# Attention times v in plain float32 on two column halves of the array, in a fused attention and MoE kernel

## The chip, the cores and the metric

The kernel runs on one core of a Trainium2 chip. The metric is device time in microseconds (us), from the start of the program to its end, taken over several runs and given as a median. A profile of one execution goes with it; its times are read from the hardware profiler's trace.

## The reference

Three layers follow each other. The change is in the first, in the last line of the first function.

```python
def _attn_ref(q, k, v):                       # (4, 12, 448, 64) each
    scores = scale * np.matmul(q, k.transpose(0, 1, 3, 2)) - np.log(S)
    attn = 1.0 / (1.0 + np.exp(-scores))      # a sigmoid, no row sum
    return np.matmul(attn, v).astype(np.float32)

def _moe_ref(x, w1, w2, w3, w_out):           # x: 1792 x 768
    h = np.maximum(np.maximum(x @ w1, x @ w2), x @ w3)
    return (h @ w_out).astype(np.float32)

def _moe2_ref(x, w_in, w_out, g_ln):          # x @ w_in: 1792 x 1024
    ...                                       # h * softmax(h), layer norm, @ w_out
```

All inputs are float32 (the weights arrive as 64-bit floats and are turned into float32 on the chip).

## The kernel before

**Precision.** TensorE multiplies here in float32r, a form of float32 with a short mantissa. To keep float32 accuracy the kernel splits an operand into a rounded part (`copy`, L50/L52) and what is left (`rest`, L55), and adds the products of the parts in PSUM.

**Attention.** There are 24 pairs of heads (`pr`), 6 for each of 4 batches. The 448 keys of a pair are cut into four chunks `c` of 128 rows; the last chunk has 64 new keys and 64 that repeat. `prep_qk` and `prep_v` split k, q and v. `scores` (L350) makes the scores of one chunk for both heads: three products (hi·hi, hi·lo, lo·hi) per head, each head on one 64-row half of the array, 6 matmuls of 448 columns. `sig` (L366) takes the sigmoid on ScalarE and writes the weights `sf`. `attn_split` (L371) splits them into `ah` and `al`; for chunk 3 the rest is written into the upper half of `ah` itself, over the repeated keys. `attend` (L384) multiplies with v: the stationary operand `vt` holds v's rounded part in 64 columns and its rest in the other 64, so that one matmul makes two products, and `ah` and `al` are streamed through it one after the other. That is 4 matmuls of 448 columns for chunks 0 to 2 (two heads, two parts) and 2 for chunk 3, 14 in all for a pair, into one PSUM tile per head. After chunk 3 the two column halves of each tile are added (`sbt` on ScalarE, L406, then `xs` on VectorE, L407), and the sum is split again into `xh` and `xl` (L411, L412) for the next layer.

**Order of the work.** TensorE's order is written out by hand in the loop at L438 over 49 half-steps `hs`: scores of two chunks, a piece of other matmuls (`fill`), `attend` of two chunks of the half-step before, another piece of fill. So there are 48 groups of `attend`, by turns 8 and 6 matmuls, each between pieces of fill. The fill is `gen_w` first (L265, tiles `pw`: the product of two weight matrices, 216 matmuls of 512 columns), and then `gen_g1` (L300, tiles `pg`: x times w1, w2, w3, 324 matmuls of 448 columns for a batch). The order on ScalarE, VectorE and the DMA queue of SyncE is made by a scheduler from the dependences. Weights are loaded as raw 64-bit data (`raw`, three buffers), turned into float32 (`to_f32`: `y`) and split (`wih`/`wil`, `r_wo`, `r_w`). After the attention come the second layer's product (`h`, L539), the norm, transposes of its result (`pt`, L572, the one plain float32 operation on TensorE) and the output product (`po`, L588).

Of the kernel before, what the change touches and what calls it, by code (L numbers as in the profile page):

```python
# [7 lines left out]
F32 = mybir.dt.float32  # L8
F32R = mybir.dt.float32r
I32 = mybir.dt.int32  # L10
AF = mybir.ActivationFunctionType
ALU = mybir.AluOpType
# [4 lines left out]
P = 128  # L17
B, H, S, D = 4, 12, 448, 64
SX = S + D
NPAIR = H // 2  # L20
# [13 lines left out]
def sigmoid_attention_max_moe_solu_ln(tc, q, k, v, w123, wo, wi, w2, g, out):  # L34
# [11 lines left out]
    pe, act, dve, pool, sp = nc.tensor, nc.scalar, nc.vector, nc.gpsimd, nc.sync  # L46

    def copy(eng, dst, src):
        if eng is act:
            act.copy(dst, src)  # L50
        else:
            eng.tensor_copy(dst, src)  # L52

    def rest(eng, dst, src, hi):
        eng.tensor_tensor(out=dst, in0=src, in1=hi.bitcast(F32), op=ALU.subtract)  # L55

    def open_pool(name, bufs, side="left", space=None):
        kw = dict(name=name, bufs=bufs, side=side)
        if space is not None:
            kw["space"] = space  # L60
        cm = tc.tile_pool(**kw)
        return cm, cm.__enter__()
# [13 lines left out]
    a_cm, apool = open_pool("apool", 2)  # L76
    ps1 = [open_pool("ps_sc", 2, space=PSUM), open_pool("ps_av", 2, space=PSUM), open_pool("ps_f", 2, space=PSUM)]
    ps_sc, ps_av, ps_f = (p for _, p in ps1)
# [13 lines left out]
    def run_bg(n=1):  # L92
        while n > 0 and bg:
            if next(bg[0], "end") == "end":
                bg.popleft()
            else:
                n -= 1
# [106 lines left out]


    NP = NPAIR * B
    qk_raw, v_raw, qk_ops, v_ops = {}, {}, {}, {}
    pq = deque()

    def run_pq(n=1):  # L210
# [13 lines left out]
    def load_v(pr):  # L224
        if pr >= NP:
            return
        vr = apool.tile([P, 2, 4, D], F32, tag="vr", name=f"vr{pr}", bufs=1)
        sp.dma_start(out=vr, in_=v[pr])
        v_raw[pr] = vr

    def prep_qk(pr):
        if pr >= NP:
            return []
        qr, kr = qk_raw.pop(pr)
        kt = apool.tile([P, 2, SX], F32R, tag="kt", name=f"kt{pr}")
        qt = apool.tile([P, 2, S], F32R, tag="qt", name=f"qt{pr}")
        qk_ops[pr] = (qt, kt)
        return [
            lambda: copy(dve, kt[:, 0], kr),
            lambda: copy(act, qt[:, 0], qr),  # L240
            lambda: rest(dve, kt[:, 1], kr, kt[:, 0]),
            lambda: rest(dve, qt[:, 1], qr, qt[:, 0]),
            lambda: load_qk(pr + 1),
        ]

    def prep_v(pr):
        if pr >= NP:
            return []
        vr = v_raw.pop(pr)
        vt = apool.tile([P, 2, 4, 2, D], F32R, tag="vt", name=f"vt{pr}")  # L250
        v_ops[pr] = vt
        return [
            lambda: copy(act, vt[:, :, :, 0], vr),
            lambda: rest(dve, vt[:, :, :, 1], vr, vt[:, :, :, 0]),
            lambda: load_v(pr + 1),
        ]


    def group(ps, terms):
# [37 lines left out]
    xs_hi, xs_lo, hts = {}, {}, {}  # L297
# [47 lines left out]
                run_bg()  # L345


    aw = {}

    def scores(pr, c):  # L350
        qt, kt = qk_ops[pr]
        sc = ps_sc.tile([P, 2, 512], F32, tag="sc", name=f"sc{pr}_{c}")
        terms = ((0, 0), (0, 1), (1, 0))
        for t, (x, y) in enumerate(terms):
            for j in range(2):
                rows = slice(j * D, (j + 1) * D)
                pe.matmul(  # L357
                    sc[:, j, :S],
                    lhsT=kt[rows, x, c * P : (c + 1) * P],
                    rhs=qt[rows, y],  # L360
                    start=(t == 0),
                    stop=(t == len(terms) - 1),
                )
        return sc

    def sig(pr, c, sc):  # L366
        sf = apool.tile([P, 2, S], F32, tag="sf", name=f"sf{pr}_{c}", bufs=2)
        act.activation(sf, sc[:, :, :S], AF.Sigmoid, bias=bias_s, scale=1.0 / math.sqrt(D))  # L368
        return sf

    def attn_split(pr, c, sf):  # L371
        ah = apool.tile([P, 2, S], F32R, tag="ah", name=f"ah{pr}_{c}", bufs=4)
        copy(dve if c == 3 and pr >= 2 * NPAIR else act, ah, sf)
        if c < 3:
            al = apool.tile([P, 2, S], F32R, tag="al", name=f"al{pr}_{c}", bufs=3)
            rest(dve, al, sf, ah)
            aw[(pr, c)] = (ah, al)
        else:
            rest(dve, ah[D:], sf[D:], ah[D:])
            aw[(pr, c)] = (ah,)  # L380

    pas = {}

    def attend(pr, c):  # L384

        b, hp = divmod(pr, NPAIR)
        vt = v_ops[pr]
        if c == 0:
            pas[pr] = [ps_av.tile([P, 512], F32, tag="av", name=f"av{pr}_{j}") for j in range(2)]
        parts = aw.pop((pr, c))  # L390
        for j in range(2):
            for i, t in enumerate(parts):
                pe.matmul(  # L393
                    pas[pr][j][:, :S],
                    lhsT=vt[:, j, c].rearrange("p a d -> p (a d)"),
                    rhs=t[:, j],
                    start=(c == 0 and i == 0),
                    stop=(c == 3),
                )
        if c < 3:  # L400
            return
        sbt = apool.tile([P, S], F32, tag="sbt", name=f"sbt{pr}", bufs=1)
        xs = apool.tile([P, S], F32, tag="xs", name=f"xs{pr}", bufs=1)
        for j, pa in enumerate(pas.pop(pr)):
            mine, other = slice(j * D, (j + 1) * D), slice((1 - j) * D, (2 - j) * D)
            act.copy(sbt[mine], pa[other, :S])  # L406
            dve.tensor_tensor(out=xs[mine], in0=pa[mine, :S], in1=sbt[mine], op=ALU.add)  # L407
        if hp == 0:
            xs_hi[b] = (xp0, xp1)[b % 2].tile([P, KC, S], F32R, tag="xh", name=f"xh{b}")
            xs_lo[b] = (xp0, xp1)[b % 2].tile([P, KC, S], F32R, tag="xl", name=f"xl{b}")  # L410
        copy(act if b < 2 else dve, xs_hi[b][:, hp], xs)  # L411
        rest(dve, xs_lo[b][:, hp], xs, xs_hi[b][:, hp])  # L412
        qk_ops.pop(pr)
        v_ops.pop(pr)
        if hp == NPAIR - 1:
            x_done.add(b)
# [8 lines left out]
    for op in prep_qk(0) + prep_v(0):  # L425
        op()
# [11 lines left out]
    for hs in range(HS + 1):  # L438
        pr, h = divmod(hs, 2)
        if hs <= 2 * NPAIR:  # L440
            total = W_MM * max(0, hs - 1) // (2 * NPAIR - 1)
        else:
            total = W_MM + RATE * (hs - 2 * NPAIR)
        todo = total - done
        done = total
        cuts = [todo * i // 4 for i in range(5)]
        parts = [cuts[i + 1] - cuts[i] for i in range(4)]
        mine = [(pr, c) for c in (2 * h, 2 * h + 1)] if hs < HS else []
        scs = [scores(*x) for x in mine]
        sfs = [sig(*x, sc) for x, sc in zip(mine, scs)]  # L450
        if hs < HS:
            pq.extend(prep_v(pr + 1) if h else prep_qk(pr + 1))
        for x, sf, n in zip(mine, sfs, parts):
            attn_split(*x, sf)
            if hs < 2:
                run_bg(9)
            run_pq(2)
            fill(n)
        if hs == HS:
            fill(sum(parts))  # L460
        if hs > 0:
            for c in (2, 3) if h == 0 else (0, 1):
                attend(pr - (h == 0), c)
        fill(parts[2])
        run_pq(len(pq))
        if hs < HS:
            fill(parts[3])
# [32 lines left out]
    n = 0  # L500
# [119 lines left out]
def _layout(i):  # L620
    import numpy as np

    def bits(a):
        return np.ascontiguousarray(a).view(np.int64)

    def pairs(a):

        return a.reshape(B * NPAIR, 2, S, D).transpose(0, 1, 3, 2).reshape(B * NPAIR, P, S)

    f = np.ascontiguousarray  # L630
    k = pairs(i["k"])
    v = i["v"].reshape(B * NPAIR, 2, S, D)
    v = np.concatenate([v, v[:, :, S - D :]], axis=2).reshape(B * NPAIR, 2, 4, P, D).transpose(0, 3, 1, 2, 4)
    w = np.stack([i["moe_w1"], i["moe_w2"], i["moe_w3"]]).reshape(3, KC, P, FC, P)
    return {
        "q": f(pairs(i["q"])),
        "k": f(np.concatenate([k, k[..., S - D :]], axis=2)),
        "v": f(v),
        "w123": bits(w.transpose(3, 0, 2, 1, 4).reshape(NG, P, U)),
        "wo": bits(i["moe_w_out"].reshape(FC, P, KC, P).transpose(0, 3, 2, 1).reshape(FC, P, U)),  # L640
        "wi": bits(
            i["moe2_w_in"].reshape(KC, P, 2, 512).transpose(2, 1, 0, 3).reshape(2, P, 4, U).transpose(0, 2, 1, 3)
        ),
        "w2": bits(i["moe2_w_out"].reshape(K2, P, DM)),
        "g": f(i["moe2_g_ln"].reshape(K2, P).T),
    }
# [19 lines left out]
```

## Time and profile before

| | |
|---|---|
| median of 3 runs | 741.26 us (740.29 to 741.61) |
| profiled execution, its span (no other time of it is recorded) | 740.2 us |
| TensorE matmuls busy | 715.0 us, 97% of the span, 3712 instructions |
| TensorE weight loads busy | 619.9 us |
| VectorE busy | 448.3 us, 734 instructions |
| ScalarE busy | 380.5 us, 596 instructions |

The profile gives, for one execution, the busy time of each engine, groups of like instructions, what each engine waited for, and the instructions in order of time. PE is TensorE, PEld its weight loads, ACT ScalarE, DVE VectorE, SPq the DMA queue of SyncE. A matmul's duration in a row contains its way through the array; how often one can follow another is read from the starts.

### The profile page before, as it was taken

What the parts mean: (1) busy time and instruction counts of PE and PEld (TensorE: products, weight loads), DVE (VectorE), ACT (ScalarE), POOL (GpSimd) and SP (SyncE); (2) the same over time, 40 slices, a digit from 0 to 9 for tenths busy, and PEclk for the clock granted to TensorE, in tenths of its full rate; (3) what the DMA queues carried; (4) which work ended last, traced back from release to release, by engine and by line L of the source; (5) the groups of instructions that cost most, each with busy time, mean ns of one, the idle gap of its engine ahead of it and who ended that gap; (6) DMA issues with size and microseconds to landing.
All of it is one profiled execution on the core that took longest, in us unless ns stands there. A gap on an engine that the chain in (4) does not pass through costs nothing.

```text
span 740.2 us, 9584 instructions
## 1 busy us (share of the span) xinstructions
PE 715.0 (97%) x3712; PEld 619.9 (84%) x3712; DVE 448.3 (61%) x734; ACT 380.5 (51%) x596; POOL 19.6 (3%) x37
## 2 busy tenths in 40 slices
PE   5699989999999999999999999999999999999998
PEld 3478767878888888888888899988999999999997
DVE  5999989999866666665555451269444444444330
ACT  6889989888865555555555250164333222222121
POOL 0010112000000000000000000000000000000000
PEclk9699999999999999999999999999999999999999
DMA  8787899888855566555543589820000000000011
GB/s 285 235 275 231 267 357 324 310 299 307 316 191 185 170 195 200 183 174 181 186 165 128 162 291 420 319 85 1 23 22 21 22 22 22 22 22 22 25 40 44
DMA packets 31438, 124.89 MB, mean 169 GB/s; under 512 B 3616, under 2 KB 6944, under 8 KB 30624
## 3 DMA queue, kind: packets, MB, share of 16 engines
q1 hardware_dynamic: 27072, 103.83, 40.8%
q0 software_dynamic: 4320, 20.45, 7.6%
q8 instruction: 29, 0.48, 0.3%
q14 instruction: 17, 0.14, 0.0%
HBM read 98.31 MB, written 25.95 MB: 168 GB/s over the span
## 4 chain that ended last, share of the span: by engine, by line
PE 78%; ACT 7%; DVE 7%; DMA 4%; issue 4%; SPq 0%; POOL 0%; DVEq 0%; ACTq 0%; POOLq 0%
PE pg L262 32%; PE po L588 16%; PE h L539 16%; PE av L393 6%; PE sc L357 6%; DMA raw<-in_wi 2%; ACT sf L368 2%; PE pt L572 2%; ACT ah L50 1%; DVE r_w L55 1%; PE pw L262 1%; DVE al L55 1%; DMA qr<-in_q 1%; DMA w_d<-ws 1%; ACT y_w L141 1%
## 5 line engine op out<-in xcount | busy, mean ns | idle before, releaser
L262 PE MATMUL pg<-xh,r 128*128 128x448 f32 x648 | 190.5, 369 | 0.0
L262 PEld LDWEIGHTS pg<-xh,r 128*128 128x128 f32 x648 | 121.7, 188 | 16.3 <-issue 4.0
L55 DVE TENSOR_TENSOR al<-sf,ah 128x896 fp32r<-128x896 f32 x72 | 78.3, 1090 | 82.3 <-ACT ah L50 82.0
L368 ACT ACTIVATE sf<-sc,bias_s 128x896 f32<-128x896 f32 x96 | 95.8, 1004 | 54.0 <-PE sc L357 54.0
L262 PE MATMUL pg<-xl,r 128*128 128x448 f32 x324 | 118.3, 365 | 0.0
L539 PE MATMUL h<-wf,hh 128*128 128x512 f32 x336 | 103.9, 390 | 0.0
L357 PE MATMUL sc<-qt,kt 64*128 64x448 f32 x576 | 76.3, 396 | 10.4 <-DVE kt L55 4.7
L50 ACT CAST ah<-sf 128x896 fp32r<-128x896 f32 x84 | 78.2, 943 | 1.7
L357 PEld LDWEIGHTS sc<-qt,kt 64*128 64x128 f32 x576 | 52.2, 192 | 30.7 <-issue 10.8
L588 PE MATMUL po<-w2h,lh 128*128 128x384 f32 x224 | 76.2, 340 | 0.0
L551 DVE TENSOR_REDUCE st<-h 128x1 f32<-128x1024 f32 x14 | 17.1, 1224 | 96.7 <-PE h L539 96.7
L588 PE MATMUL po<-w2h,ll 128*128 128x384 f32 x224 | 75.2, 336 | 0.0
L588 PE MATMUL po<-w2l,lh 128*128 128x384 f32 x224 | 75.2, 336 | 0.0
L539 PEld LDWEIGHTS h<-wf,hh 128*128 128x128 f32 x336 | 62.8, 188 | 12.5
L393 PE MATMUL av<-ah,vt 128*128 128x448 f32 x192 | 68.5, 377 | 0.4 <-DVE xs L407 0.4
L262 PE MATMUL pg<-xh,r_w 128*128 128x448 f32 x216 | 65.2, 373 | 0.5 <-DVE ws L55 0.5
L539 PE MATMUL h<-wf,hl 128*128 128x512 f32 x168 | 65.6, 391 | 0.0
L262 PEld LDWEIGHTS pg<-xl,r 128*128 128x128 f32 x324 | 60.9, 188 | 4.5
L262 PE MATMUL pw<-wih,r_wo 128*128 128x512 f32 x144 | 48.2, 411 | 8.0 <-ACT r_wo L50 5.8
L50 ACT CAST hh<-h 128x128 fp32r<-128x128 f32 x84 | 18.3, 296 | 72.4 <-PE h L539 70.5
L393 PE MATMUL av<-al,vt 128*128 128x448 f32 x144 | 53.6, 372 | 0.9 <-DVE al L55 0.9
L325 ACT COPY s<-pg 128x448 f32<-128x448 f32 x24 | 12.8, 534 | 71.8 <-PE pg L262 71.8
(81 smaller groups left out, 1013.4 us busy)
## 6 DMA issues: line engine op xcount, KB each, us to landing
r<-w_d SPq DMA_DIRECT2D x54, 768.0 KB, 4.4
raw<-in_w SPq DMA_DIRECT2D x26, 768.0 KB, 6.3
w_d<-r_w POOLq DMA_DIRECT2D x18, 768.0 KB, 4.7
kr<-in_k SPq DMA_DIRECT2D x24, 256.0 KB, 2.8
raw<-in_wi SPq DMA_DIRECT2D x8, 768.0 KB, 6.5
vr<-in_v SPq DMA_DIRECT2D x24, 256.0 KB, 3.0
w_d<-ws POOLq DMA_DIRECT2D x12, 512.0 KB, 4.6
wf<-w_d SPq DMA_DIRECT2D x6, 1024.0 KB, 9.8
```

What stands on the lines that cost most here:

```text
L50: act.copy(dst, src)
L55: eng.tensor_tensor(out=dst, in0=src, in1=hi.bitcast(F32), op=ALU.subtract)
L141: act.activation(y, raw.bitcast(F32)[:, :, 1], AF.Prelu, scale=2.0**-112, alpha=2.0**32)
L262: pe.matmul(ps, lhsT=l, rhs=r, start=(i == 0), stop=(i == n - 1))
L325: act.copy(s[:, :S], ps[:, :S])
L357: pe.matmul(sc[:, j, :S], lhsT=kt[rows, x, c * P : (c + 1) * P], rhs=qt[rows, y], start=(t == 0), stop=(t == len(terms) - 1),)
L368: act.activation(sf, sc[:, :, :S], AF.Sigmoid, bias=bias_s, scale=1.0 / math.sqrt(D))
L393: pe.matmul(pas[pr][j][:, :S], lhsT=vt[:, j, c].rearrange("p a d -> p (a d)"), rhs=t[:, j], start=(c == 0 and i == 0), stop=(c == 3),)
L539: pe.matmul(ps[:, n], lhsT=l, rhs=r, start=(f == 0 and i == 0), stop=(f == FC - 1 and i == 2))
L551: dve.tensor_reduce(out=nmax, in_=ps, axis=AX.XY, op=ALU.max, negate=True)
L572: pe.transpose(ps[:, kc], u[:, kc * P : (kc + 1) * P], ident)
L588: pe.matmul(ps[:, :hw], lhsT=l, rhs=r, start=(kc == 0 and i == 0), stop=(kc == K2 - 1 and i == 2))
```

## The change

`attend` takes v as it was loaded (`vr`) and the sigmoid's output `sf` as it was written, both plain float32. Each head's matmul has 64 stationary columns and writes one half (64 partitions) of a single PSUM tile, so both heads of the pair share a tile and each has one column half of the array. There are 2 matmuls for each chunk, 8 for a pair. The splits of v and of the weights, and the sum of the two column halves, are gone; `xh` and `xl` are made from PSUM, `xh` always on ScalarE. `vr` has three buffers in place of one, `sf` five in place of two. The repeated rows of v are zeros now.

```diff
     def load_v(pr):
...
-        vr = apool.tile([P, 2, 4, D], F32, tag="vr", name=f"vr{pr}", bufs=1)
+        vr = apool.tile([P, 2, 4, D], F32, tag="vr", name=f"vr{pr}", bufs=3)
...
     def prep_v(pr):
-        vt = apool.tile([P, 2, 4, 2, D], F32R, tag="vt", name=f"vt{pr}")
-        return [
-            lambda: copy(act, vt[:, :, :, 0], vr),
-            lambda: rest(dve, vt[:, :, :, 1], vr, vt[:, :, :, 0]),
-            lambda: load_v(pr + 1),
-        ]
+        return [lambda: load_v(pr + 1)]
...
-        sf = apool.tile([P, 2, S], F32, tag="sf", name=f"sf{pr}_{c}", bufs=2)
+        sf = apool.tile([P, 2, S], F32, tag="sf", name=f"sf{pr}_{c}", bufs=5)
...
-    def attn_split(pr, c, sf):
-        ah = apool.tile([P, 2, S], F32R, tag="ah", name=f"ah{pr}_{c}", bufs=4)
-        copy(dve if c == 3 and pr >= 2 * NPAIR else act, ah, sf)
-        if c < 3:
-            al = apool.tile([P, 2, S], F32R, tag="al", name=f"al{pr}_{c}", bufs=3)
-            rest(dve, al, sf, ah)
-            aw[(pr, c)] = (ah, al)
-        else:
-            rest(dve, ah[D:], sf[D:], ah[D:])
-            aw[(pr, c)] = (ah,)
...
     def attend(pr, c):
...
-            pas[pr] = [ps_av.tile([P, 512], F32, tag="av", name=f"av{pr}_{j}") for j in range(2)]
+            pas[pr] = ps_av.tile([P, 512], F32, tag="av", name=f"av{pr}")
+        pa = pas[pr]
+        sf = weights.pop((pr, c))
         for j in range(2):
-            for i, t in enumerate(parts):
-                pe.matmul(
-                    pas[pr][j][:, :S],
-                    lhsT=vt[:, j, c].rearrange("p a d -> p (a d)"),
-                    rhs=t[:, j],
-                    start=(c == 0 and i == 0),
-                    stop=(c == 3),
-                )
+            pe.matmul(pa[j * D : (j + 1) * D, :S], lhsT=vr[:, j, c], rhs=sf[:, j], start=(c == 0), stop=(c == 3))
...
-        for j, pa in enumerate(pas.pop(pr)):
-            mine, other = slice(j * D, (j + 1) * D), slice((1 - j) * D, (2 - j) * D)
-            act.copy(sbt[mine], pa[other, :S])
-            dve.tensor_tensor(out=xs[mine], in0=pa[mine, :S], in1=sbt[mine], op=ALU.add)
...
-        copy(act if b < 2 else dve, xs_hi[b][:, hp], xs)
-        rest(dve, xs_lo[b][:, hp], xs, xs_hi[b][:, hp])
+        pas.pop(pr)
+        copy(act, xs_hi[b][:, hp], pa[:, :S])
+        rest(dve, xs_lo[b][:, hp], pa[:, :S], xs_hi[b][:, hp])
```

On TensorE, a group of `attend` with chunks 2 and 3 of a pair, in the middle of the attention. Before (number behind a name: the buffer; `pg` is fill, `x2` two matmuls of the same tiles):

```order
L262 MATMUL pg_5_2485<-xh_1309,r_5_2270 128x448 x2
L393 MATMUL av_0_2412<-ah_2_2384,vt_2224 128x448
L393 MATMUL av_0_2412<-al_2_2386,vt_2224 128x448
L393 MATMUL av_1_2413<-ah_2_2384,vt_2224 128x448
L393 MATMUL av_1_2413<-al_2_2386,vt_2224 128x448
L393 MATMUL av_0_2412<-ah_3_2400,vt_2224 128x448
L393 MATMUL av_1_2413<-ah_3_2400,vt_2224 128x448
L262 MATMUL pg_5_2485<-xl_1310,r_5_2270 128x448
```

The same place now (`64x448` is the output, 64 partitions of one tile for each head):

```order
L253 MATMUL pg_5_2048<-xl_1082,r_5_1872 128x448
L253 MATMUL pg_5_2048<-xh_1081,r_5_1872 128x448 x2
L371 MATMUL av_1988<-sf_2_1965,vr_1714 64x448 x2
L371 MATMUL av_1988<-sf_3_1967,vr_1714 64x448 x2
L253 MATMUL pg_5_2048<-xl_1082,r_5_1872 128x448
```

Six or eight matmuls have become four, head 0 then head 1 of each chunk, at the same place among the fill.

On ScalarE near the start, where the first piece `r_wo` of the weights for the fill is made (`qt` is the copy of the q of the pair after next, which needs its load). Before:

```order
L141 ACTIVATE y_wo_220<-raw_163 128x768
L368 ACTIVATE sf_0_260<-sc_0_246,bias_s 128x896
L50 CAST wih_2_179<-y_wi_3_183 128x768
L50 CAST ah_0_266<-sf_0_260 128x896
L50 CAST qt_265<-qr_190 128x448
L50 CAST r_wo_226<-y_wo_220 128x768
```

And now:

```order
L359 ACTIVATE sf_0_234<-sc_0_220,bias_s 128x896
L359 ACTIVATE sf_1_236<-sc_1_227,bias_s 128x896
L50 CAST wih_2_168<-y_wi_3_172 128x768
L141 ACTIVATE y_wo_204<-raw_156 128x768
L141 ACTIVATE y_wo_245<-raw_166 128x768
L50 CAST r_wo_210<-y_wo_204 128x768
L50 CAST qt_239<-qr_179 128x448
```

`r_wo` stood behind that `qt` and stands ahead of it now; the copies `ah` between them are gone.

## Rows read from the trace of the kernel before

**Rows 1.** The page: busy time and share of each engine; TensorE's granted clock by slices.

```profile
PE 715.0 (97%) x3712; PEld 619.9 (84%) x3712; DVE 448.3 (61%) x734; ACT 380.5 (51%) x596; POOL 19.6 (3%) x37
PEclk9699999999999999999999999999999999999999
```

**Rows 2.** Busy time by stretch: us; PE, PEld, DVE, ACT, POOL; PE clock, DMA share, GB/s.

```profile
0.00:40.00 40.00, 23.63 (x90) 16.47 (x91) 30.18 (x43) 30.62 (x40) 1.59 (x8) 0.83 0.73 251
40.00:108.00 68.00, 63.97 (x318) 48.63 (x317) 63.53 (x87) 59.62 (x82) 7.49 (x11) 1.00 0.85 289
108.00:200.00 92.00, 90.80 (x479) 74.38 (x477) 83.28 (x113) 78.07 (x106) 10.52 (x18) 1.00 0.86 310
200.00:425.00 225.00, 225.00 (x1209) 194.89 (x1208) 133.09 (x186) 121.19 (x156) 0.00 (x0) 1.00 0.55 178
```

**Rows 3.** Waits of PE, 0 to 40 us: us in total, times, longest.

```profile
PE pw L262 <- ACT r_wo L50: 5.6, 2, 5.3
PE sc L357 <- DVE kt L55: 4.7, 1, 4.7
PE sc L357 <- ACT sf L368: 3.2, 2, 2.8
PE sc L357 <- DVE qt L55: 2.1, 1, 2.1
```

**Rows 4.** Waits of PE from 40 us to the end, the three longest of eight.

```profile
PE pw L262 <- DVE ws L55: 1.5, 1, 1.5
PE pw L262 <- DVE wil L55: 1.2, 1, 1.2
PE pw L262 <- DVE r_wo L55: 0.7, 1, 0.7
```

**Rows 5.** Groups of instructions: the matmuls of attend, xcount, busy us, mean ns.

```profile
L393 PE MATMUL av<-ah,vt 128*128 128x448 f32 x192 | 68.5, 377 | 0.4 <-DVE xs L407 0.4
L393 PE MATMUL av<-al,vt 128*128 128x448 f32 x144 | 53.6, 372 | 0.9 <-DVE al L55 0.9
```

**Rows 6.** Timeline of PE (start, us): first of eight matmuls of attend; what follows them.

```profile
40.38 0.37 PE L393 MATMUL av<-ah,vt 128*128 128x448 f32 x1
...
42.02 0.39 PE L262 MATMUL pw<-wih,r_wo 128*128 128x512 f32 x1
```

**Rows 7.** Timeline of PE around a group of scores, two heads on two row halves.

```profile
198.30 0.37 PE L262 MATMUL pg<-xh,r_w 128*128 128x448 f32 x1
198.60 1.49 PE L357 MATMUL sc<-qt,kt 64*128 64x448 f32 x12
200.01 0.47 PE L262 MATMUL pg<-xh,r_w 128*128 128x448 f32 x1
200.32 0.37 PE L262 MATMUL pg<-xl,r_w 128*128 128x448 f32 x1
```

**Rows 8.** Timeline of PE: eight transposes in plain float32, and what follows.

```profile
513.16 1.03 PE L572 MATMUL pt<-ident,u 128*128 128x128 f32 x8
513.96 0.47 PE L539 MATMUL h<-wf,hh 128*128 128x512 f32 x1
```

**Rows 9.** Groups on ACT and DVE, 0 to 440 us: the split of the weights.

```profile
L50 ACT CAST ah<-sf 128x896 fp32r<-128x896 f32 x84 | 78.2, 943 | 1.7
...
L55 DVE TENSOR_TENSOR al<-sf,ah 128x896 fp32r<-128x896 f32 x72 | 78.3, 1090 | 82.3 <-ACT ah L50 82.0
```

**Rows 10.** The chain of waits near the start: start us, us, what.

```profile
20.13 6.13 DMA qr<-in_q
...
26.84 0.74 ACT r_wo L50
...
27.63 4.21 PE pw L262 x9
```

**Rows 11.** Timeline of SP's DMA queue: loads issued after vr came free.

```profile
11.13 0.33 SPq L228 DMA_DIRECT2D vr<-in_v  x1
...
11.98 0.42 SPq L133 DMA_DIRECT2D raw<-in_wi  x1
```

More of the change, by code (lines that the diff above doesn't have):

```diff
@@ L206, in sigmoid_attention_max_moe_solu_ln @@
     NP = NPAIR * B
-    qk_raw, v_raw, qk_ops, v_ops = {}, {}, {}, {}
+    qk_raw, qk_ops, v_ops = {}, {}, {}
     pq = deque()
@@ L226, in load_v @@
             return
-        vr = apool.tile([P, 2, 4, D], F32, tag="vr", name=f"vr{pr}", bufs=1)
+        vr = apool.tile([P, 2, 4, D], F32, tag="vr", name=f"vr{pr}", bufs=3)
         sp.dma_start(out=vr, in_=v[pr])
-        v_raw[pr] = vr
+        v_ops[pr] = vr
     def prep_qk(pr):
@@ L246, in prep_v @@
     def prep_v(pr):
-        if pr >= NP:
-            return []
-        vr = v_raw.pop(pr)
-        vt = apool.tile([P, 2, 4, 2, D], F32R, tag="vt", name=f"vt{pr}")
-        v_ops[pr] = vt
-        return [
-            lambda: copy(act, vt[:, :, :, 0], vr),
-            lambda: rest(dve, vt[:, :, :, 1], vr, vt[:, :, :, 0]),
-            lambda: load_v(pr + 1),
-        ]
+        return [lambda: load_v(pr + 1)]
     def group(ps, terms):
@@ L345, in fill @@
                 run_bg()
-    aw = {}
     def scores(pr, c):
@@ L364, in scores @@
         return sc
+    weights, pas = {}, {}
     def sig(pr, c, sc):
-        sf = apool.tile([P, 2, S], F32, tag="sf", name=f"sf{pr}_{c}", bufs=2)
+        sf = apool.tile([P, 2, S], F32, tag="sf", name=f"sf{pr}_{c}", bufs=5)
         act.activation(sf, sc[:, :, :S], AF.Sigmoid, bias=bias_s, scale=1.0 / math.sqrt(D))
-        return sf
-    def attn_split(pr, c, sf):
-        ah = apool.tile([P, 2, S], F32R, tag="ah", name=f"ah{pr}_{c}", bufs=4)
-        copy(dve if c == 3 and pr >= 2 * NPAIR else act, ah, sf)
-        if c < 3:
-            al = apool.tile([P, 2, S], F32R, tag="al", name=f"al{pr}_{c}", bufs=3)
-            rest(dve, al, sf, ah)
-            aw[(pr, c)] = (ah, al)
-        else:
-            rest(dve, ah[D:], sf[D:], ah[D:])
-            aw[(pr, c)] = (ah,)
-    pas = {}
+        weights[(pr, c)] = sf
     def attend(pr, c):
         b, hp = divmod(pr, NPAIR)
-        vt = v_ops[pr]
+        vr = v_ops[pr]
         if c == 0:
-            pas[pr] = [ps_av.tile([P, 512], F32, tag="av", name=f"av{pr}_{j}") for j in range(2)]
-        parts = aw.pop((pr, c))
+            pas[pr] = ps_av.tile([P, 512], F32, tag="av", name=f"av{pr}")
+        pa = pas[pr]
+        sf = weights.pop((pr, c))
         for j in range(2):
-            for i, t in enumerate(parts):
-                pe.matmul(
-                    pas[pr][j][:, :S],
-                    lhsT=vt[:, j, c].rearrange("p a d -> p (a d)"),
-                    rhs=t[:, j],
-                    start=(c == 0 and i == 0),
-                    stop=(c == 3),
-                )
+            pe.matmul(pa[j * D : (j + 1) * D, :S], lhsT=vr[:, j, c], rhs=sf[:, j], start=(c == 0), stop=(c == 3))
         if c < 3:
             return
-        sbt = apool.tile([P, S], F32, tag="sbt", name=f"sbt{pr}", bufs=1)
-        xs = apool.tile([P, S], F32, tag="xs", name=f"xs{pr}", bufs=1)
-        for j, pa in enumerate(pas.pop(pr)):
-            mine, other = slice(j * D, (j + 1) * D), slice((1 - j) * D, (2 - j) * D)
-            act.copy(sbt[mine], pa[other, :S])
-            dve.tensor_tensor(out=xs[mine], in0=pa[mine, :S], in1=sbt[mine], op=ALU.add)
         if hp == 0:
@@ L449, in sigmoid_attention_max_moe_solu_ln @@
         scs = [scores(*x) for x in mine]
-        sfs = [sig(*x, sc) for x, sc in zip(mine, scs)]
+        for x, sc in zip(mine, scs):
+            sig(*x, sc)
         if hs < HS:
             pq.extend(prep_v(pr + 1) if h else prep_qk(pr + 1))
-        for x, sf, n in zip(mine, sfs, parts):
-            attn_split(*x, sf)
+        for _, n in zip(mine, parts):
             if hs < 2:
@@ L632, in _layout @@
     v = i["v"].reshape(B * NPAIR, 2, S, D)
-    v = np.concatenate([v, v[:, :, S - D :]], axis=2).reshape(B * NPAIR, 2, 4, P, D).transpose(0, 3, 1, 2, 4)
+    v = np.concatenate([v, np.zeros_like(v[:, :, S - D :])], axis=2).reshape(B * NPAIR, 2, 4, P, D).transpose(0, 3, 1, 2, 4)
     w = np.stack([i["moe_w1"], i["moe_w2"], i["moe_w3"]]).reshape(3, KC, P, FC, P)
```

## The prediction

> **What bounds the kernel now.** I read the shares of the engines first, then the stretches, then TensorE's waits, and last the starts of its matmuls. TensorE is busy 97% of the span and its clock is granted in full but for two slices at the start [rows 1]; full is the 2.4 GHz level, and the low slice holds the first matmuls, which are scattered. By stretch [rows 2] there are three regimes. From 200 to 425 us matmuls fill all of the 225 us, while VectorE has 133 and ScalarE 121: nothing that the change takes off those two can show there. From 40 to 200 us TensorE is idle 68 − 63.97 = 4.0 and 92 − 90.80 = 1.2 us, with VectorE at 63.5 of 68 and 83.3 of 92 close behind. Only in the first 40 us is TensorE idle for long, 40 − 23.63 = 16.4 us. So the change is judged by what it does to TensorE's own time in 48 groups of attend, and what it gives back is bounded by 16.4 + 5.2 us.
>
> **What a group costs now.** The rows of attend count 192 + 144 = 336 matmuls [rows 5]. Their durations overlap, so the price is read from starts: eight of them begin at 40.38 and the next operation at 42.02 [rows 6], 0.205 us each. 336 × 0.205 = 68.9 us, by 48 groups 1.435 us each. They need no change of the array's shape against the fill around them.
>
> **What a group will cost: three unknowns.** The trace has no plain float32 product and no matmul on a column half.
>
> *One matmul.* The nearest rows are the transposes, plain float32 too: eight of 128 columns in 513.96 − 513.16 = 0.80 us [rows 8], 0.78 ns per column against 0.205 / 448 = 0.46, so 448 columns would take 0.35 us if the array went over them once. That is the low bound. It moves numbers and multiplies nothing, though. The high bound comes from the attend rows: before, a head and chunk takes two matmuls, each with v's parts in the two column halves, which is four products of 64 columns. An unsplit operand has the same bits, and an array that takes short mantissas in one go has the same four products to make, now on 64 columns only: 4 × 0.205 = 0.82 us. I take 0.82, as the matmuls of attend [rows 5] do the same arithmetic and the transposes do not. I read the transposes [rows 8] as what one pass over unsplit data costs, about twice a float32r pass, so I expect two passes of 2 × 0.205 = 0.41 us. The Trainium skill (FP8 and Floating Point Precision, TensorE Precision Notes) says that a true float32 product is four passes through the array; by it the estimate is 0.82 us, by the transposes' row alone 0.35, and no row before the change decides it.
>
> *Two heads at once.* The scores' rows show halves of rows at work together: twelve matmuls begin at 198.60 and the next operation at 200.01 [rows 7], 1.41 us where twelve in turn would need 2.46. I expect column halves to do the same, but in the order in which they are issued: head 0's two passes, head 1's two, and so on. The second pass of one head and the first pass of the next overlap; the two passes of one head cannot, as they use the same columns. Four matmuls are then a chain of 4 + 1 = 5 passes: 5 × 0.41 = 2.05 us. Bounds: 4 passes' time (1.64) if all overlaps, 8 (3.28) if nothing does.
>
> *Changing the shape.* Around the scores' group, 198.30 to 200.32 is 2.02 us [rows 7]; one fill matmul, six pairs and one fill matmul at 0.205 would be 1.64. The remaining 0.38 us is what entering and leaving the halved array costs. Each attend group will now do that too; bounds 0 and 0.38, and I take 0.38, since nothing in the code distinguishes the two.
>
> Sum for a group: 2.05 + 0.38 − 1.435 = +0.995 us; × 48 = **+47.8 us**, all of it on the path wherever TensorE is the bound, which after this change is everywhere past 40 us.
>
> **What is given back.** Gone are 84 copies of 943 ns on ScalarE and 72 differences of 1090 ns on VectorE, 78 us on each [rows 9], and the smaller splits of v and sums of halves. Past 200 us the fill hides it all; the cover stays, since the fill's matmuls are untouched. Between 40 and 200 us the waits are for operands that VectorE made late [rows 4]; with longer half-steps and a lighter VectorE I let 4 of the 5.2 us go (bounds 0 and 5.2). In the first 40 us [rows 3] the 4.7 us for `kt` stay: that is the first load and two operations that the change leaves alone. The 5.3 us for `r_wo`: the chain [rows 10] shows a load of q until 26.26, ScalarE held by its copy, and `r_wo` queued behind it, then the first fill at 27.63. In the new order `r_wo` is ahead of that copy, and the raw weights' load, which stood in SP's queue behind the load of v (issued at 11.13, as soon as its one buffer was free, and the raw load at 11.98 [rows 11]), no longer waits for that buffer. What is late next is the raw load itself. I let 3 of the 5.3 go, and 3 of the 3.2 + 2.1 us for `sf` and `qt`, since a copy and up to two differences leave the queue ahead of each. Against that the first attend groups run while the granted clock is at the 1.2 GHz level and cost about 1 us more: net −5 us (bounds 0 and −12). Together **−9 us**, bounds 0 and −17.
>
> The new reads of PSUM by `xh` and `xl` follow the group as `sbt` and `xs` did, with two operations fewer, and TensorE needs them only at the next batch: nothing. The single tile for a pair leaves a second one free, so the next pair does not wait for it. Five `sf` hold two half-steps and one more: no new wait, because the group that frees them is earlier in TensorE's order than the scores that need them. The zeros for the repeated keys are made outside the measured time.
>
> Sum: 740.2 + 47.8 − 9 = 779.0 us for this execution's span; the median of the runs shown lies 1.1 us above it, so **780 us**. With the give-back at its bounds, 772 to 789.
>
> **Rivals.**
> - *All overlaps.* The two heads run side by side for the whole group: 4 × 0.41 + 0.38 − 1.435 = +0.585, × 48 = 28.1, less 9: 760 us. For it: the scores' pairs start together. Against: two passes of one instruction come one behind the other. The Trainium skill (TensorE: Matmul & The Clock Gate, Measured speedup vs the span model) has column tiles start about 4 ns apart and end together; by that rule it would be this case, and the trace shows it for row halves only. Chance 0.13.
> - *Nothing or little overlaps.* Column halves take turns, so the change doesn't do what its shape is for: 8 × 0.41 + 0.38 − 1.435 = +2.225, × 48 = 106.8, less 9: 839 us. Four short passes for each matmul that overlap only at the seams give 13 × 0.205 + 0.38 − 1.435 = +1.61, × 48 = 77.3, less 9: 810 us. For it: both heads stream all 128 rows, which the scores' halves never do, and write one PSUM tile. Together 0.30 (839: 0.22, 810: 0.08).
> - *Faster.* A plain float32 matmul is one pass at the transposes' price and the heads overlap: 2 × 0.35 + 0.38 − 1.435 = −0.355, × 48 = −17.0, less 9: 715 us. It decides if a matmul follows another within 0.5 us. For it: the transposes [rows 8]. Against: the four products. Chance 0.09.
> - *No change.* Full overlap and no cost for changing the shape: 4 × 0.41 − 1.435 = +0.205, × 48 = 9.8, less 9: 742 us. Chance 0.04.
>
> **How the numbers follow.** Forecast 0.44, then 0.13, 0.30, 0.09 and 0.04. Within 0.2% is about what a measurement of this kernel can tell from no change. Faster 0.09, same 0.04, slower 0.87. The range leaves out the faster and the unchanged case (0.13) and a little at each end: from 754, the full overlap with more given back than I took, to 842, no overlap; the forecast alone would be 768 to 790.
>
> **What would show it.** Each step has its place in the new profile. Attend's rows: if there are two matmul rows for each instruction, 384, and starts 0.41 us apart, the passes are as I say; heads that begin 0.82 apart with no overlap are the 839 case, pairs that start together the 760 case, 0.35 the faster one. From the last fill matmul ahead of a group to the second behind it should be 2.05 + 0.38 + 0.41 = 2.84 us. ScalarE and VectorE should each lose over 80 us of busy time, and TensorE should be idle less than 2 us between 40 us and the end. The first fill should begin 3 to 6 us before 27.63. Wrong would be a group that takes less than 1.4 us, or idle time of TensorE past 40 us that grows.

## The result: 1.1% slower, and outside the forecast

The changed kernel takes **749.34 us** (749.26 to 750.60, 4 runs) against 741.43 us before (740.29 to 741.68, 4 runs): a ratio of 1.0108, 95% interval 1.0089 to 1.0127. The direction is as forecast; the time is under the stated range of 754 to 842 us, and of the 39 us that it was to cost, 8 came.

The page of the changed kernel, busy times as in [rows 1], and the busy time by stretch, columns as in [rows 2]:

```profile
PE 729.8 (98%) x3760; PEld 577.5 (77%) x3760; DVE 295.9 (40%) x542; ACT 273.4 (37%) x452; POOL 19.4 (3%) x37
```

```profile
0.00:40.00 40.00, 26.09 (x108) 15.32 (x109) 29.88 (x43) 27.25 (x35) 1.59 (x8) 0.87 0.88 314
40.00:108.00 68.00, 68.00 (x341) 43.52 (x340) 38.67 (x56) 41.35 (x55) 8.80 (x13) 1.00 0.82 295
108.00:200.00 92.00, 92.00 (x480) 65.23 (x479) 47.07 (x67) 47.91 (x63) 9.01 (x16) 1.00 0.82 294
200.00:425.00 225.00, 225.00 (x1181) 162.73 (x1181) 42.98 (x71) 65.93 (x86) 0.00 (x0) 1.00 0.53 166
```

VectorE lost 152 us and ScalarE 107, and TensorE is busy without a gap from 40 us on, as forecast. All waits of TensorE that are left lie at the start (waits of PE, whole span; us, times, longest):

```profile
PE pw L253 <- ACT r_wo L50: 5.3, 1, 5.3
PE sc L346 <- DVE kt L55: 4.7, 1, 4.7
PE sc L346 <- ACT sf L359: 2.3, 1, 2.3
PE sc L346 <- DVE qt L55: 1.1, 1, 1.1
PE sc L346 <- ACT qt L50: 0.6, 1, 0.6
```

These rows answer to [rows 3]; those of [rows 4] are gone. The wait for `r_wo` is as long as before (5.3 us), but it ends earlier. The first fill:

```profile
24.34 2.93 PE L253 MATMUL pw<-wih,r_wo 128*128 128x512 f32 x6 [5.30 <-ACT r_wo L50]
```

That is 3.3 us ahead of the 27.63 of before [rows 10].

What a group of attend costs is in these rows: the groups of attend's instructions (the answers to [rows 5]), and TensorE's timeline around one group.

```profile
L371 PE MATMUL av<-sf,vr 128*64 128x448 f32 x384 | 84.3, 561 | 0.0
L371 PEld LDWEIGHTS av<-sf,vr 128*64 128x64 f32 x384 | 23.7, 138 | 38.8 <-issue 38.8
```

```profile
332.01 0.57 PE L253 MATMUL pg<-xh,r 128*128 128x448 f32 x2
332.51 1.72 PE L371 MATMUL av<-sf,vr 128*64 128x448 f32 x8
334.17 0.47 PE L253 MATMUL pg<-xl,r 128*128 128x448 f32 x1
334.47 0.36 PE L253 MATMUL pg<-xh,r 128*128 128x448 f32 x1
```

192 instructions are 384 rows: each plain float32 matmul is two loads and two passes. The group's eight passes start within the 1.66 us from 332.51 to 334.17; one after the other at 0.376 us, they would need 3.0. From 332.01 to 334.47 is 2.46 us, less three fill matmuls at 0.203 is 1.85 us for the group with its borders, where the prediction had 2.43. In the trace the eight rows start in four pairs, 6 or 7 ns apart within a pair, 0.43 us from the first pair to the second and 0.376 after that: 4 × 0.376 = 1.50 us of passes and 0.35 us at the borders. The loads of the stationary operands, which run ahead of them, show the same pairs (timeline of PEld; the first row is two pairs, 0.05 us apart, the second of them loaded while the first pair of passes runs):

```profile
332.51 0.20 PEld L371 LDWEIGHTS av<-sf,vr 128*64 128x64 f32 x4 [0.31 <-issue]
332.94 0.14 PEld L371 LDWEIGHTS av<-sf,vr 128*64 128x64 f32 x2 [0.23 <-issue]
333.32 0.14 PEld L371 LDWEIGHTS av<-sf,vr 128*64 128x64 f32 x2 [0.23 <-issue]
```

So the balance over the program is seen where the half-steps begin. The first scores of half-steps 3, 22 and 47, after:

```profile
32.84 0.69 PE L346 MATMUL sc<-qt,kt 64*128 64x448 f32 x4
...
193.79 0.47 PE L346 MATMUL sc<-qt,kt 64*128 64x448 f32 x2
...
417.89 0.67 PE L346 MATMUL sc<-qt,kt 64*128 64x448 f32 x3
```

Before, half-steps 3 and 47 (half-step 22 is the row at 198.60 of [rows 7]):

```profile
36.55 0.47 PE L357 MATMUL sc<-qt,kt 64*128 64x448 f32 x2
...
411.72 0.48 PE L357 MATMUL sc<-qt,kt 64*128 64x448 f32 x2
```

At half-step 3 the changed kernel is 3.7 us ahead, at 22 it is 4.8 ahead, at 47 it is 6.2 behind. From 22 to 47 it loses 11.0 us in 25 half-steps. The new groups stand there for 13 groups of six matmuls and only 12 of eight, which makes 0.2 us of it, so an average group costs 0.43 us more: that is its price where TensorE alone decides, and × 48 it is 20.6 us. The span grew by 747.6 − 740.2 = 7.4. So **13.2 us came back**, some 4 of it before half-step 3 and 9 between 3 and 22.

### The profile page after: what moved, and what is told of

Its sections match the earlier page's. It is cut to its first block, busy times and chain, and to the rows that moved or that the text cites. A ratio compares the mean times of both kernels' runs of the same rounds, so it can differ in the third digit from the quotient of the medians.

```text
span 747.6 us, 9355 instructions
## 1 busy us (share of the span) xinstructions
PE 729.8 (98%) x3760; PEld 577.5 (77%) x3760; DVE 295.9 (40%) x542; ACT 273.4 (37%) x452; POOL 19.4 (3%) x37
## 4 chain that ended last, share of the span: by engine, by line
PE 96%; ACT 1%; DMA 1%; DVE 1%; issue 0%; SPq 0%
PE pg L253 37%; PE po L555 16%; PE h L506 15%; PE av L371 10%; PE sc L346 9%; PE pw L253 8%; PE pt L539 2%; DMA raw<-in_wi 1%; ACT sf L359 1%; ACT wih L50 0%; DVE wil L55 0%; ACT y_wi L141 0%; DVE y_wo L147 0%; ACT r_wo L50 0%; DVE y_wo L144 0%
## 5 line engine op out<-in xcount | busy, mean ns | idle before, releaser
L253 PE MATMUL pg<-xl,r 128*128 128x448 f32 x324 | 120.9, 373 | 0.0
L359 ACT ACTIVATE sf<-sc,bias_s 128x896 f32<-128x896 f32 x96 | 92.2, 1006 | 75.5 <-PE sc L346 75.5
L371 PE MATMUL av<-sf,vr 128*64 128x448 f32 x384 | 84.3, 561 | 0.0
L346 PE MATMUL sc<-qt,kt 64*128 64x448 f32 x576 | 74.5, 390 | 8.6 <-DVE kt L55 4.7
L318 DVE TENSOR_TENSOR s<-pg,s 128x448 f32<-128x448 f32 x24 | 15.0, 625 | 156.4 <-PE pg L253 155.3
L371 PEld LDWEIGHTS av<-sf,vr 128*64 128x64 f32 x384 | 23.7, 138 | 38.8 <-issue 38.8
L253 PEld LDWEIGHTS pg<-xh,r_w 128*128 128x128 f32 x216 | 40.5, 188 | 6.8 <-issue 3.7
```

The lines of the kernel that those rows point to most:

```text
L253: pe.matmul(ps, lhsT=l, rhs=r, start=(i == 0), stop=(i == n - 1))
L318: dve.tensor_tensor(out=s[:, :S], in0=ps[:, :S], in1=s[:, :S], op=ALU.max)
L346: pe.matmul(sc[:, j, :S], lhsT=kt[rows, x, c * P : (c + 1) * P], rhs=qt[rows, y], start=(t == 0), stop=(t == len(terms) - 1),)
L371: pe.matmul(pa[j * D : (j + 1) * D, :S], lhsT=vr[:, j, c], rhs=sf[:, j], start=(c == 0), stop=(c == 3))
```

## The experiments

Two questions: which passes run side by side, and where the 13 us came from. Theories A to E are named in the expectations; the letters A and B of the first question are not those of the second. Beside a time of several runs stands the 95% interval of its ratio to the kernel before on the same chip.

### Which passes overlap: the order, the half, the full array

`head_major`: the four matmuls of a group in another order.

```diff
-        for j in range(2):
-            pe.matmul(pa[j * D : (j + 1) * D, :S], lhsT=vr[:, j, c], rhs=sf[:, j], start=(c == 0), stop=(c == 3))
+        for j in range(2):
+            for c, sf in zip(cs, sfs):
+                pe.matmul(pa[j * D : (j + 1) * D, :S], lhsT=vr[:, j, c], rhs=sf[:, j], start=(c == 0), stop=(c == 3))
```

> Each group of four matmuls goes head 0 of both chunks, then head 1 of both, instead of by turns. Theory A: the passes that start together in the trace (8 rows in 4 pairs, 0.376 us apart) are one of each head, and they are found only among neighbours in the order. Then the two heads overlap at one seam, 7 passes instead of 4: 3 x 0.376 = 1.13 us more for each of 48 groups, 54 us, so about 803. Theory B: the rows that start together are the two passes of one matmul. Then the order is of no account: 749. If the heads overlap but TensorE looks further ahead in its queue, 749 too, and the run with both heads on one column half decides between these two.

Measured: 750.7 us, one run (before: 741.1). The order is of no account, and it did change: in every pair of rows from half-step 4 on the second starts 13 or 14 ns behind the first, where the changed kernel has 6 or 7. Timeline of TensorE:

```profile
172.13 1.73 PE L372 MATMUL av<-sf,vr 128*64 128x448 f32 x8
173.79 0.47 PE L253 MATMUL pg<-xl,r_w 128*128 128x448 f32 x1
```

`same_half`: both heads on partitions 0 to 63, each in a PSUM tile of its own.

```diff
-            pe.matmul(pa[j * D : (j + 1) * D, :S], lhsT=vr[:, j, c], rhs=sf[:, j], ...)
+            pe.matmul(pa[j][:D, :S], lhsT=vr[:, j, c], rhs=sf[:, j], ...)
```

> Both heads write partitions 0 to 63, each into a PSUM tile of its own, so both use the same column half. Theory A (heads side by side): 8 passes in turn instead of 4, 4 x 0.376 = 1.50 us more for each of 48 groups, 72 us, about 821; a second copy and difference for each pair on ScalarE and VectorE are hidden. Theory B (the two passes of one matmul side by side): 749, as now.

Measured: 821.5 us, one run. Theory A to the microsecond. Timeline:

```profile
186.85 3.22 PE L371 MATMUL av<-sf,vr 128*64 128x448 f32 x8
190.00 0.47 PE L253 MATMUL pg<-xl,r_w 128*128 128x448 f32 x1
```

The group takes 190.00 − 186.85 = 3.15 us instead of 1.66. On one column half no two passes overlap, so the pairs seen in the changed kernel are one pass of each head, and theory B is out. With `head_major` it also follows that a pass of head 1 starts beside the first pass of head 0 although three other passes of head 0 come before it in the order: each column half takes the next pass that is for it.

`full_array`: both heads' v in 128 stationary columns (v is laid out for it), each head streamed through alone into a PSUM tile of its own, half of which is used.

```diff
-            pe.matmul(pa[j * D : (j + 1) * D, :S], lhsT=vr[:, j, c], rhs=sf[:, j], ...)
+            pe.matmul(pa[j][:, :S], lhsT=vr[:, c].rearrange("p a d -> p (a d)"), rhs=sf[:, j], ...)
```

> The stationary operand holds both heads' v in 128 columns; each head streams through it into its own PSUM tile and half of each tile is not used. No change of the array's shape against the fill. Theory A: 8 passes in turn at twice the 0.205 us of a float32r matmul, 3.28 us for a group, against 1.65 + 0.20 at its borders now: +1.43 x 48 = 69, about 818, and no extra time at the groups' borders. Theory B: 4 passes, 1.64 us and no border: about 739.

Measured: 801.9 us, one run: theory A again, but 16 us less than it had expected. Timeline:

```profile
178.86 3.17 PE L371 MATMUL av<-sf,vr 128*128 128x448 f32 x8
181.52 0.71 PE L253 MATMUL pg<-xl,r_w 128*128 128x448 f32 x1
182.07 0.36 PE L253 MATMUL pg<-xh,r_w 128*128 128x448 f32 x1
```

The eight passes start 0.376 us apart here too, not 0.41, and half-steps are 10.12 us long where the kernel before has 8.53, 1.59 more: a group costs 1.435 + 1.59 = 3.03 us, and 8 × 0.376 is 3.01, so there is nothing at its borders. A pass over plain float32 is 0.376 us for 448 columns at 64 stationary columns and at 128, and the 0.35 us at the borders belong to the halved array.

### The borders: fewer changes of shape

`one_group`: all four chunks of a pair in one group.

```diff
-            for c in (2, 3) if h == 0 else (0, 1):
-                attend(pr - (h == 0), c)
+            for c in range(4) if h == 0 else ():
+                attend(pr - 1, c)
```

> All four chunks of a pair in one group of attend, 24 groups instead of 48; sf has seven buffers. Now a group is 4 x 0.376 = 1.50 us of passes and 0.35 us at its borders (0.10 before the first, 0.05 at the second, 0.10 at the last, 0.10 behind the next fill matmul). If the borders are paid once for each change of shape, 24 x 0.35 = 8 us go: about 741. If they are a part of the passes themselves, 749. If the weights that wait longer hold up the sigmoids, more than 749.

Measured: 742.73 us (ratio to before 1.0019, 1.0006 to 1.0031), 6.6 us under the changed kernel. Timeline:

```profile
212.26 0.56 PE L253 MATMUL pg<-xh,r_w 128*128 128x448 f32 x2
212.76 3.23 PE L371 MATMUL av<-sf,vr 128*64 128x448 f32 x16
215.91 0.47 PE L253 MATMUL pg<-xl,r_w 128*128 128x448 f32 x1
216.22 0.37 PE L253 MATMUL pg<-xh,r_w 128*128 128x448 f32 x1
```

From 212.26 to 216.22, less three fill matmuls, is 3.35 us for sixteen passes with their borders, against 2 × 1.85 for two groups of eight: 8 × 0.376 is 3.01, so the 0.35 us at the borders are paid once for each group.

`one_group_next`: the same group right behind the scores, with no fill between.

> As one_group, and the group of attend stands right behind the scores, with no full-array matmul between. If a border is paid for each change of the array's shape, row halves straight to column halves saves one of the two changes around each group: 24 x 0.2 = 5 us, about 738. If leaving one half shape for the other costs as much as going through the full array, 742.7 as one_group. Rival: attend now waits for the sigmoids of the half-step before less long behind them, and TensorE idles: above 743.

Measured: 741.63 us (0.9991 to 1.0016). The gain is not shown: the intervals of the two overlap. Around a group the timeline does show one:

```profile
208.14 0.37 PE L253 MATMUL pg<-xh,r_w 128*128 128x448 f32 x1
208.44 1.50 PE L346 MATMUL sc<-qt,kt 64*128 64x448 f32 x12
209.86 3.23 PE L371 MATMUL av<-sf,vr 128*64 128x448 f32 x16
213.02 0.47 PE L253 MATMUL pg<-xh,r_w 128*128 128x448 f32 x1
213.33 0.36 PE L253 MATMUL pg<-xl,r_w 128*128 128x448 f32 x1
```

The group begins 1.42 us after the scores, as the fill does elsewhere (1.41, [rows 7]), and pays no entry of its own: from 208.14 to 213.33, less two fill matmuls, is 4.78 us, where the scores and the group apart cost 1.61 [rows 7] and 3.35. So one of the two changes is saved, 0.18 us for each group, as expected. But from half-step 22 on the half-steps without a group are 0.12 us longer than in `one_group` (7.19 against 7.08 us): their fill matmuls start 0.207 us apart there and 0.203 in `one_group`. Why is not known; it takes back more than half of what is saved.

### Where the 13 us came from

For these runs a table of starts in one execution each: scores of half-step 3 and of half-step 22, read from each timeline, the time between, and how much of it is left over the shortest of the kernels (`no_split_ws2`, 152.5 us) when the TensorE work that was added in these 19 half-steps is taken off (8.2 us for column halves, 10 × 0.81 for the spare matmuls).

| kernel | half-step 3 | half-step 22 | between | left over |
|---|---|---|---|---|
| before | 36.55 | 198.60 | 162.05 | 9.5 |
| changed | 32.84 | 193.79 | 160.95 | 0.2 |
| `no_split` | 34.04 | 193.31 | 159.27 | 6.8 |
| `no_split_ws2` | 33.08 | 185.59 | 152.51 | 0 |
| `before_ws2` | 35.72 | 197.02 | 161.30 | 8.8 |
| `split_kept` | 35.04 | 196.23 | 161.19 | 0.5 |
| `before_spare` | 36.56 | 205.75 | 169.19 | 8.6 |
| `no_split_spare` | 34.62 | 198.92 | 164.30 | 3.7 |

Executions of the kernel before lie between 739.0 and 743.6 us on these chips, so a difference of 1 or 2 us in the last column says little.

`no_split`: the kernel before without the split of the attention weights. The sigmoid writes float32r into five buffers, the weights' low part is left out, and in chunk 3 the repeated keys count twice.

```diff
-        ah = apool.tile([P, 2, S], F32R, tag="ah", name=f"ah{pr}_{c}", bufs=4)
...
+        aw[(pr, c)] = (sf, sf) if c < 3 else (sf,)
```

> The kernel before with its 336 float32r matmuls in their order, but the sigmoid writes float32r and that is streamed twice; the copies and differences that split the weights (78 us on ScalarE, 112 us on VectorE) are gone, and the low part of the weights is left out of the result. Theory A: the changed kernel pays 48 x 0.41 = 20 us on TensorE and gets 12 us back from the lighter ScalarE and VectorE before 200 us. Then this run shows the second alone: 741 - 10 to 13, about 730. Rival C: what came back is due to v's three buffers and the loads that moved ahead. Then about 740 here, because v is loaded and split as before.

Measured: 739.84 us (0.9969 to 0.9994), 1.2 us less than before and not 10 to 13. Theory A falls as it stood: a lighter ScalarE and VectorE alone give back next to nothing. One of ScalarE's waits from 33 to 200 us, a piece of the chain of waits and two of TensorE's waits say why:

```profile
ACT ws L50 <- DMA w_d<-ws: 21.2, 6, 7.6
```

```profile
77.01 0.68 DVE ws L55
...
78.09 7.31 DMA w_d<-ws
...
85.50 0.59 ACT ws L50
```

```profile
PE pw L262 <- DVE ws L55: 3.0, 3, 1.9
PE av L385 <- DVE xs L399: 0.6, 1, 0.6
```

`ws`, the finished piece of the weight product (L292 of the kernel before), has one buffer. ScalarE stands before the next copy into it until the store of the last has landed, 7.31 us after its issue. What TensorE then waits for is `ws` itself, whose copy has to free a PSUM tile before a further `pw` can be written, and `xs`, the sum of the halves, whose ScalarE part stands behind that copy. In the kernel before, ScalarE stood only 0.5 us for that store from 33 to 200 us.

`no_split_ws2`: the same with `bufs=2` for `ws`.

> As no_split, with two buffers in place of one for ws, the product of the two weight matrices on its way to memory. In no_split ScalarE stood up to 7.6 us before the copy into ws until the store of the one before had landed, and the sigmoids behind it were late. Theory D (the first 200 us are paced by such waits, not by the engines' load): the 6 us that no_split still loses between half-steps 3 and 22 go, 739.8 - 4 to 6, about 735. Rival: the next wait in line (the raw weights' loads) takes its place: 739 to 740.

Measured: 732.06 us (0.9863 to 0.9896), 8 us less than `no_split`. No wait of TensorE shows between 33 and 200 us, so this is taken as the whole of the time between half-steps 3 and 22 that waits can give back.

`before_ws2`: the kernel before with that buffer alone.

> The kernel before with two buffers for ws (and s cut to the 448 columns that are used, for the room). Theory D: part of the 9 us lost between half-steps 3 and 22 was the wait for that store: 741 - 2 to 5, 736 to 739. If ScalarE and VectorE's load is what counts in the kernel before, 741.

Measured: 739.89 us (0.9967 to 0.9996), 1.2 us less than before. TensorE no longer waits for `ws`. Past 33 us it waits 0.8 us for a sigmoid, and for the weights that VectorE and ScalarE prepare:

```profile
PE pw L262 <- DVE wil L55: 1.2, 1, 1.2
PE pw L262 <- DVE r_wo L55: 0.8, 1, 0.8
PE pw L262 <- ACT wih L50: 0.6, 1, 0.6
```

The kernel before has waits of both kinds [rows 4], `no_split` hardly any but those for `ws` and `xs`. Each remedy alone gives 1.2 us, both together 9: two chains one behind the other, and whichever is removed, the other takes its place.

`split_kept`: the changed kernel with the old split of the weights still computed (with two buffers for `ah` and one for `al`), its result read by nobody.

> The changed kernel with the old split of the weights still done on ScalarE and VectorE and read by nobody (the split of v and the sum of the halves stay out). Theory A: the give-back goes, all but the part of v and the sums: 749.3 + 6 to 12, about 758; TensorE idles between 40 and 200 us again. Rival C: 749 to 751.

Measured: 752.04 us (1.0137 to 1.0171), 2.7 us more than the changed kernel, where 6 to 12 were expected. TensorE still has no gap between 40 and 200 us (busy by stretch, columns as in [rows 2]):

```profile
40.00:108.00 68.00, 68.00 (x337) 42.95 (x335) 59.77 (x79) 57.19 (x75) 8.25 (x12) 1.00 0.84 302
108.00:200.00 92.00, 92.00 (x484) 66.14 (x481) 70.18 (x91) 68.59 (x86) 9.54 (x17) 1.00 0.83 300
```

VectorE and ScalarE are at 59.8 and 57.2 of 68 us, close to the 63.5 and 59.6 of before, and TensorE waits for neither. Here the copies and differences are done, but attend does not need them; 2.2 of the 2.7 us are lost before half-step 3 (35.04 against 32.84).

`before_spare`: the kernel before with TensorE's added work and nothing else.

```diff
+            for _ in range(2 if c == 0 else 0):
+                pe.matmul(pas[pr][j][:, :S], lhsT=vt[:, j, c]..., rhs=parts[0][:, j], start=True, stop=True)
```

> The kernel before with four spare matmuls for each pair (the first product of each head two times more, overwritten by what follows), 4 x 0.203 = 0.81 us for a pair, 19.5 us in all, the same that the change adds to TensorE for a pair; nothing is taken from ScalarE and VectorE. Theory D: before half-step 22 TensorE loses 9 us between its matmuls to waits that are not TensorE's, and added TensorE work there is hidden in them. Then only the 13 pairs behind it count, 10.6 us, and at most 2 more: 752 to 754. Theory A (only a lighter ScalarE and VectorE make room): all of it counts, 760.

Measured: 757.81 us (1.0203 to 1.0249), between the two and nearer to A. Of 8.1 us added between half-steps 3 and 22, 7.1 show in the profiled execution, the slowest of four (759.87); by the medians 16.7 of all 19.5 us show. Theory D, that longer half-steps alone cover the waits, falls too. TensorE waits for `ws` and for `xs`:

```profile
PE pw L262 <- DVE ws L55: 3.2, 2, 1.6
PE av L393 <- DVE xs L409: 2.5, 2, 2.2
```

`no_split_spare`: both.

> no_split with the spare matmuls of before_spare: the weights' split is gone from ScalarE and VectorE and TensorE has 0.81 us more for a pair, as in the changed kernel, but by float32r matmuls on the full array. Theory E (two chains held TensorE up before half-step 22, the load of ScalarE and VectorE and the single buffer for ws; a lighter load removes the first and longer half-steps hide the second, each alone leaves the other): the 6 us that no_split loses there are mostly hidden, so 739.8 + 10.6 for the 13 later pairs + 2 to 4, 752 to 754. If the two only add up (before_spare hid 1 us of the spare work), 739.8 + 18 = 758.

Measured: 755.81 us (1.0166 to 1.0221), again between: the waits left over are 3.7 us, fewer than either alone leaves (6.8 and 8.6), and more than the 0.2 of the changed kernel. Theory E has the direction right and not the whole size. From 33 to 200 us TensorE waits 1.6 us for `ws` and 0.7 for `xs`; the changed kernel, which has no `xs`, waits for neither, though ScalarE stands 18.6 us there for the store of `ws`. The spare matmuls come in every second half-step, the changed kernel's added work in each; whether that is the difference was not tried.

`v_one_buffer`: the changed kernel with `bufs=1` for `vr`.

> The changed kernel with one buffer for v in place of three. SyncE's queue now holds the next v until attend has read the last, and the weights' loads behind it wait too. Rival C (the give-back comes from loads that moved ahead): up to 9 us are lost, 752 to 758. Theory D: TensorE covers a late load: 749 to 751.

Measured: 750.23 us (1.0109 to 1.0139), not distinguishable from the changed kernel (1.0089 to 1.0127), and half-step 3 begins at 32.90: the buffers of v are not where the time came from. The loads that moved ahead are not tested by this run, because with one buffer the scheduler put the second load of v behind the weights' first loads (raw weights issued at 9.98, 10.56 in the changed kernel, 11.98 before). `no_split_ws2` tests them: v and the raw weights are loaded there as before (11.45 and 12.30), and half-step 3 begins at 33.08 all the same, with nothing lost behind it. So rival C is out.

### A version that beats both

`hyb7_one`: plain float32 on column halves, in one group for a pair, for the first 7 pairs; the other 17 as before.

```diff
+        if pr < PLAIN:
+            v_ops[pr] = vr
+            return [lambda: load_v(pr + 1)]
...
+        if pr < PLAIN:
+            return attend_plain(pr, c)
```

> Plain float32 on column halves, four chunks in one group, for the first 7 pairs; the other 17 pairs as in the kernel before. At half-step 14 the run one_group was 7.3 us ahead of the kernel before. Theory A: from there on this run keeps that lead less what the returning split costs while weights are still prepared, up to 2 us: 734 to 736. Rival: with VectorE at 83 of 92 us between 108 and 200 us the split returns at the worst place and eats the lead: 739 to 741.

Measured: **734.86 us** (0.9901 to 0.9930). Half-steps 14 and 22 begin at

```profile
120.44 0.47 PE L364 MATMUL sc<-qt,kt 64*128 64x448 f32 x2
...
190.80 0.47 PE L364 MATMUL sc<-qt,kt 64*128 64x448 f32 x2
```

against 198.60 before for the second [rows 7]: 7.8 us ahead, and 7.3 at the end of these two executions; by the medians 6.2. The lead is taken where float32r's preparation held TensorE up, and the price of plain float32 is not paid past that.

`hyb7_one_ws2`: the same with two buffers for `ws`.

> hyb7_one with two buffers for ws. Theory E: hyb7_one has the lighter load in the first 7 pairs and its half-steps are 0.17 us shorter than the changed kernel's, so ws holds it up again; with the second buffer another 1 to 3 us go: 732 to 734. If nothing waits for ws there, 734.9.

Measured: 735.04 us (0.9889 to 0.9936): nothing more. The weight product ends with half-step 12, while the plain pairs still run, and their half-steps cover it.

## Why the prediction was wrong

**The bound and the price of a pass: right.** TensorE decides past 40 us, as forecast, and each plain float32 matmul is two passes: the 384 rows are there. A pass was put at 0.41 us and is 0.376: 4 × 0.034 × 48 = 6.5 us. The four products on 64 columns were the right bound (0.82 us against 2 × 0.376); the transposes' 0.35 us [rows 8] is near one pass by luck, there are two.

**The step that failed: "the second pass of one head and the first pass of the next overlap", a chain of five passes.** The heads overlap throughout: the eight passes of a group take the time of four, in the pairs that the prediction had named as the sign of its 760 case. `same_half` shows that the heads are what overlaps, `head_major` that their order in the queue does not matter. The order of issue does not bind the two halves to each other, and I had no row for assuming that it does: the scores' pairs [rows 7] start together, but they are single passes and alternate, so they could not show it. One pass less for each group is 0.41 × 48 = 19.7 us, the largest part of the miss. The Trainium skill (TensorE: Matmul & The Clock Gate, The mechanism) has matmuls start strictly in program order. For passes on different column halves `head_major` does not agree, with 1.66 us for a group where the order of its queue would give seven passes, 7 × 0.376 = 2.6 us. The rival "all overlaps" is the case that came, with 760 us worked out for it and a chance of 0.13; the 11 us between 760 and 749 are the terms below and the size of a pass above.

**Changing the shape: right.** 0.38 us assumed, 0.35 measured, and `full_array` shows that a group without the change pays none. The three corrections (19.7 + 6.5 + 1.4) take the +47.8 us to +20.2, and half-steps 22 to 47 show 20.6.

**What is given back: 9 us predicted, 13 measured; the place past 40 us was mis-sized.** I bounded it by TensorE's idle time between 40 and 200 us, 5.2 us [rows 2], and took 4. The starts show 9. Busy time hides such gaps: a matmul's row lasts 0.37 us and its successor could start after 0.203, so a wait of up to 0.16 us does not count as idle, and one longer counts that much too little. The first 40 us gave about 4 where I had a net 5, but not by the steps I named. The wait for `r_wo`, of which 3 us were to go, is still 5.3, and the raw weights' load is not what counts (`no_split_ws2`); the scores ahead of it came earlier, the ten behind the wait for `qt` at 17.62 instead of 20.12. I also misread the clock's row [rows 1]: one slice is below full, not two (18.5 to 37 us), and the first matmuls, at 4.7 us, are not in it.

**Why it came back: only in part settled.** I credited the lighter VectorE. The runs show that the stretch was held by at least two chains, the preparation of the weights on ScalarE and VectorE and the one buffer of `ws`, and that lifting one leaves the other. `split_kept` shows that the time the split takes is not the point either: with the split still done but not awaited, TensorE does not wait. Removed there with the dependence are the split of v, the sum of the halves and the two buffers of `sf` that are five now. The five buffers alone are not it, as `no_split` has them and loses 6.8 us. The sum of the halves is a part of it: the waits for `xs` (0.6 us in `no_split`, 2.5 in `before_spare`) are gone. How the 9 us divide between these and the longer half-steps stays open.

## What to carry to other kernels

How much of an engine's time is lost to waits is read from the starts of its instructions against their undisturbed spacing; busy shares understate it when rows overlap. Where two chains pace a stretch, each remedy tried alone looks worthless: here 1.2 and 1.2 us alone, 9 together. And a costlier operation that needs no preparation can pay in the stretch where preparation is the bound, while it loses where TensorE alone decides (0.43 us a group here): mixed by stretch it gave 0.8%.

## What was not expected of the hardware

Two column halves of the array worked through their own passes out of the order of issue: head 0's four passes ahead of head 1's in the queue, and still four pairs in 1.66 us. A pass of 448 columns over plain float32 took 0.376 us at 64 and at 128 stationary columns alike, less than two float32r matmuls of the fill (0.406). And going from row halves straight to column halves took no longer than going from row halves to the full array, 1.42 us from the first of the scores to the group in `one_group_next` and 1.41 to the fill [rows 7], so that the second change, into the column halves, cost nothing.
